# Two key tiles share one column-tiled pass for the second weighted sum of an attention backward

## The chip, the cores and the metric

One core of one Trainium2 chip runs the whole program in one launch. The metric is the device time in microseconds (us). The engines are TensorE (PE, with its weight loads shown apart as PEld), VectorE (DVE), ScalarE (ACT), GpSimd (POOL), and SyncE (SP), which here only issues DMAs.

## The reference

The program computes a forward pass and its vector-Jacobian product. The forward mixes two attentions over x (2048 tokens, width 576) with a gate:

```
q = (x @ wq) in 32 heads of 18;  k = x @ wk;  v = x @ wv      # one k and v for all heads
a = softmax(q k^T / sqrt(18)) v, heads joined, @ wo           # "A": multi-query attention
b = segment-recurrent attention with 8 memory tokens          # "B": 64 segments of 32 tokens, 32 heads of 128
out = g * a + (1 - g) * b,   g = sigmoid(x . gate_w)
```

The outputs are `out` and the gradients to x, to A's four weights, to B's memory and four weights and to the gate. For A's backward each query row needs the row sum l of its exponentials E = exp(s), the output o = (sum E v)/l, and delta = (sum E dP)/l with dP = dO v^T. The gradient to q is made from sum E dP k and sum E k. So with W = E * dP, element by element, each block of queries needs five sums over all 2048 keys: E times v, 1 and k, and W times 1 and k.

## The kernel before, in words

The stages run one after another: preparation and projections, a forward weave, B's backward in bulk, a backward weave, the weight gradients, and A's last products. The change is in the forward weave.

**The weave** (`weave`, L211) keeps the order of the code on each engine: it advances the chain by one piece, then the sweep by one step, 1024 times. The chain (`b_chain_fwd`, L237) is B's recurrence: 64 segments in 16 pieces each. Counted from 0, the pieces are: the k projection in two halves (0, 1), the transposes of k (2), the q projection (3, 4), the transposes of q (5), half of v (6), scores (7), their sums (8), the other half of v and the normalised weights c_pn (9), the transposes of v (10), weights times v with c_PB (11), and four pieces for the new memory (12 to 15). All pieces share two PSUM banks of one buffer each, c_pj and c_x. A projection half goes to c_pj and is evacuated by ACT (L63); the transposed k and q go to c_x and are evacuated by ACT (c_kmT, L308) and by DVE (c_qT, L334).

**The sweep** (`a_pass1`, L1372) goes over 64 blocks (16 pairs of heads x 4 groups of 512 queries) and, in each, over 16 key tiles of 128: 1024 steps, n = 0 to 1023. A step issues:

- the scores a_S of the next key tile for the pair's two heads (two row-tiled matmuls of 32 x 512; one buffer of two banks);
- a_dP for this key tile (two matmuls, two one-bank buffers in all);
- ACT's exponential of the next tile (a_E, L1394);
- two DVE products, one for each head, a_W = a_dP * a_E (L1424);
- the weighted sum of the step before's a_W into a_acc, and that of this step's a_E.

A weighted sum (`acc_mm`, L1396) is four matmuls, each with 32 weight columns and a 32-column group of the array of its own, so that the four run side by side:

```
for g in range(4):
    self.mm(acc[32 * g:32 * g + 32, :], lhsT=st[:, n % 16, 32 * (g % 2):32 * (g % 2) + 32],
            rhs=t[:, g // 2, :], start=first, stop=last, tp=(0, 32 * g))
```

The group g = 2 * head + half. The weights have 64 columns for a key tile, taken in two halves of 32: VK holds v, a column of ones and k (37 columns used), WK holds ones and k in columns 37 to 55. So WK's first half is all zeros, and E's and W's sums add into one accumulator of 64 rows for each head. a_acc has two buffers of one bank.

At a block's end (step n % 16 = 0 of the next block) ACT copies a_acc to SBUF (a_acs, L1429), and a generator `a_post` (L1453) goes on in three parts: at n % 16 = 1, four f32 transposes of a_acs to c_pj and ACT's copy a_tk; at 4, four transposes of the queries to c_pj and ACT's copy a_qt; at 6, a reciprocal on DVE, a row of small GpSimd operations, and three stores. All of it lies in the engines' queues in this order, between the chain's pieces.

Of the kernel before, what the change touches and what calls it, by code (L numbers as in the profile page):

```python
# [7 lines left out]
ALU = mybir.AluOpType  # L8
AX = mybir.AxisListType
BF16 = mybir.dt.bfloat16  # L10
F32 = mybir.dt.float32
P = 128
# [12 lines left out]
DA = 18  # L25
# [5 lines left out]
class Kern:  # L31
# [1142 lines left out]
    def setup_A_dram(self, dram):  # L1174
        T = self.T
        self.qd_dram = dram.tile([NPR, P, T], BF16, name="qd_dram")
        self.sd_dram = dram.tile([NPR, P, self.NTT, P], BF16, name="sd_dram")
        self.kv_dram = dram.tile([P, T], BF16, name="kv_dram")
        self.vk_dram = dram.tile([2, P, self.NTT, 64], BF16, name="vk_dram")
        self.dqtok_dram = dram.tile([T, D], BF16, name="dqtok_dram")  # L1180
        self.otok_dram = dram.tile([T, NKT * P], BF16, name="otok_dram")
        self.dkv_dram = dram.tile([P, T], BF16, name="dkv_dram")

    def setup_A_consts(self, pool):
        nc = self.nc
        om = pool.tile([P, 1], F32, name="a_onesrow")
        idx = [[0, 1]]
        nc.gpsimd.memset(om[:], 0.0)
        for r in (18, 50, 82, 83, 114, 115):
            nc.gpsimd.affine_select(out=om[:], in_=om[:], compare_op=ALU.not_equal, fill=1.0,  # L1190
                                    base=-r, pattern=idx, channel_multiplier=1)
        self.onesrow = om
        sel = pool.tile([P, 36], BF16, name="a_selkv")
        nc.gpsimd.memset(sel[:], 0.0)
        for i in range(4):
            w = i // 2
            nc.gpsimd.affine_select(out=sel[:, 18 * w:18 * w + DA], in_=sel[:, 18 * w:18 * w + DA],
                                    compare_op=ALU.not_equal, fill=1.0, base=-32 * i, pattern=[[-1, DA]],
                                    channel_multiplier=1)
        self.selkv = sel  # L1200

    def prep(self, keep, xk, sp, psum):
        nc = self.nc
# [90 lines left out]
    def a_setup(self, keep, sp, psum):  # L1294
        nc = self.nc
        T, NTT = self.T, self.NTT
        KV = keep.tile([P, T], BF16, name="a_KV")
        for lo in range(0, T, 512):
            pk = psum.tile([P, 512], F32, name="a_p1", bufs=2)
            for kt in range(NKT):  # L1300
                self.mm(pk[:, :], lhsT=self.wkv[:, kt, :], rhs=self.xT[:, kt, lo:lo + 512],
                        start=(kt == 0), stop=(kt == NKT - 1))
            nc.vector.tensor_scalar(out=KV[:, lo:lo + 512], in0=pk[:, :], scalar1=self.onesrow[:, 0:1],
                                    scalar2=None, op0=ALU.add)
        self.KV = KV
        nc.sync.dma_start(self.kv_dram[:, :], KV[:, :])
        absk = sp.tile([64, T], BF16, name="a_absk", bufs=1)
        nc.scalar.activation(absk[:, :], KV[0:64, :], ACT.Abs)
        mk = sp.tile([64, 1], F32, name="a_mk", bufs=1)
        nc.vector.tensor_reduce(out=mk[:, :], in_=absk[:, :], axis=AX.X, op=ALU.max)  # L1310
        sm = keep.tile([P, 64], BF16, name="a_smneg")
        nc.gpsimd.memset(sm[:], 0.0)
        for i in range(2):
            nc.gpsimd.memset(sm[32 * i:32 * i + DA, 32 * i + DA:32 * i + DA + 1], -1.0)
        nc.vector.tensor_scalar(out=sm[0:64, :], in0=sm[0:64, :], scalar1=mk[:, 0:1], scalar2=None, op0=ALU.mult)
        self.smneg = sm
        self.VK = keep.tile([P, NTT, 64], BF16, name="a_VK")
        self.WK = keep.tile([P, NTT, 64], BF16, name="a_WK")
        nc.gpsimd.memset(self.VK[:], 0.0)
        nc.vector.memset(self.WK[:], 0.0)  # L1320
        nc.gpsimd.memset(self.VK[:, :, DA:DA + 1], 1.0)
        nc.vector.memset(self.WK[:, :, 37:38], 1.0)
        for t4 in range(NTT // 4):
            pkv = psum.tile([P, 4, 36], F32, name="a_p2", bufs=2)
            for j in range(4):
                tt = t4 * 4 + j
                for kt in range(NKT):
                    rows = KT_ROWS[kt]
                    self.mm(pkv[:, j, :], lhsT=self.xT[0:rows, kt, tt * P:(tt + 1) * P],
                            rhs=self.wkv36[0:rows, kt, :], start=(kt == 0), stop=(kt == NKT - 1))  # L1330
            tts = slice(t4 * 4, t4 * 4 + 4)
            nc.vector.tensor_copy(self.VK[:, tts, 0:DA], pkv[:, :, DA:36])
            nc.vector.tensor_copy(self.VK[:, tts, 19:37], pkv[:, :, 0:DA])
            nc.scalar.copy(self.WK[:, tts, 38:56], pkv[:, :, 0:DA])
        nc.sync.dma_start(self.vk_dram[0], self.VK[:])
        nc.gpsimd.dma_start(self.vk_dram[1], self.WK[:])

    def load_A_kv(self, keep):
        nc = self.nc
        self.KV = keep.tile([P, self.T], BF16, name="l_KV")  # L1340
        nc.sync.dma_start(self.KV[:], self.kv_dram[:, :])
        self.VK = keep.tile([P, self.NTT, 64], BF16, name="l_VK")
        nc.sync.dma_start(self.VK[:], self.vk_dram[0])
        self.WK = keep.tile([P, self.NTT, 64], BF16, name="l_WK")
        nc.sync.dma_start(self.WK[:], self.vk_dram[1])

    def a_qd_all(self, sp, psum):
        prev = None
# [23 lines left out]
    def a_pass1(self, keep, sp, psum, xps):  # L1372
        nc = self.nc
        T, NTT = self.T, self.NTT
        NB = NPR * (T // 512)
        dl_all = keep.tile([P, NTT, NPR, 2, 2], BF16, name="a_dl")
        QD, S, E_, W_ = {}, {}, {}, {}
# [15 lines left out]
            E_[n] = sp.tile([P, 2, 512], BF16, name="a_E", bufs=2)  # L1393
            nc.scalar.activation(E_[n][:], S.pop(n)[:], ACT.Exp, scale=SCALEA)  # L1394

        def acc_mm(acc, n, src, st, first, last):  # L1396
            t = src.pop(n) if src is W_ else src[n]
            for g in range(4):
                self.mm(acc[32 * g:32 * g + 32, :], lhsT=st[:, n % 16, 32 * (g % 2):32 * (g % 2) + 32],
                        rhs=t[:, g // 2, :], start=first, stop=last, tp=(0, 32 * g))  # L1400

        load(0)
        load(1)
        mm_S(0)
        ex(0)
        NP_ = 16 * NB
        acc = None
        post = None
        for n in range(NP_ + 1):
            if n < NP_:  # L1410
                kt = n % 16
                if kt == 8:
                    load(n // 16 + 2)
                if n + 1 < NP_:
                    mm_S(n + 1)
                dP = [psum.tile([P, 512], F32, name="a_dP", bufs=2) for _ in range(2)]
                for i in range(2):
                    r = slice(64 + 32 * i, 96 + 32 * i)
                    self.mm(dP[i][:], lhsT=self.KV[r, kt * P:kt * P + P], rhs=QD[n // 16][r, :], tp=(64 + 32 * i, 0))
                if n + 1 < NP_:  # L1420
                    ex(n + 1)
                W_[n] = sp.tile([P, 2, 512], BF16, name="a_W", bufs=2)
                for i in range(2):
                    nc.vector.tensor_tensor(out=W_[n][:, i, :], in0=dP[i][:], in1=E_[n][:, i, :], op=ALU.mult)  # L1424
            if n > 0:
                acc_mm(acc, n - 1, W_, self.WK, False, n % 16 == 0)
                if n % 16 == 0:
                    acs = sp.tile([P, 512], F32, name="a_acs", bufs=1)
                    nc.scalar.copy(acs[:], acc[:])  # L1429
                    bb = n // 16 - 1  # L1430
                    post = self.a_post(bb // 4, bb % 4, acs, QD.pop(bb), sp, xps, dl_all)
            if n < NP_:
                if n % 16 == 0:
                    acc = psum.tile([P, 512], F32, name="a_acc", bufs=2)
                acc_mm(acc, n, E_, self.VK, n % 16 == 0, False)
            if post is not None and n % 16 in (1, 4, 6):
                if next(post, "end") == "end":
                    post = None
            yield
# [10 lines left out]
                    nc.sync.dma_start(self.qd_dram[p][82 + 32 * i:84 + 32 * i, t4 * 512:(t4 + 1) * 512],  # L1450
                                      dlT[4 * p + 2 * i:4 * p + 2 * i + 2, :])

    def a_post(self, p, qb, acs, QD, sp, psum, dl_all):  # L1453
        nc = self.nc
        pt = psum.tile([P, 4, P], F32, name="c_pj", bufs=1)
        for j in range(4):
# [3 lines left out]
        ptf = pt[:].rearrange("p a b -> p (a b)")  # L1460
        nc.scalar.copy(tkf, ptf)
        yield
        pd = psum.tile([P, 4, P], BF16, name="c_pj", bufs=1)
        for j in range(4):
            self.tr(pd[:, j, :], QD[:, j * P:(j + 1) * P], P)
# [4 lines left out]
        nc.vector.reciprocal(rl[:, :, 1, :], tk[:, :, :, 18])  # L1470
        nc.gpsimd.tensor_scalar(out=rl[:, :, 0, :], in0=rl[:, :, 1, :], scalar1=SCALEA, scalar2=None, op0=ALU.mult)
        dl = sp.tile([P, 4, 2], F32, name="a_d", bufs=2)
        nc.gpsimd.tensor_tensor(out=dl[:], in0=tk[:, :, :, 37], in1=rl[:, :, 1, :], op=ALU.mult)
        tts = slice(4 * qb, 4 * qb + 4)
        hi = sp.tile([P, 4, 2], BF16, name="a_dh", bufs=2)
        nc.gpsimd.tensor_scalar(out=hi[:], in0=dl[:], scalar1=-1.0, scalar2=None, op0=ALU.mult)
# [10 lines left out]
        nc.sync.dma_start(otd(self.otok_dram), ot[:].rearrange("p a b c -> p a (b c)"))  # L1487
        t1 = sp.tile([P, 4, 2, DA], F32, name="a_t1", bufs=1)
        nc.gpsimd.tensor_tensor(out=t1[:], in0=tk[:, :, :, 19:37], in1=bc(dl[:], DA), op=ALU.mult)
        nc.gpsimd.tensor_tensor(out=t1[:], in0=tk[:, :, :, 38:56], in1=t1[:], op=ALU.subtract)  # L1490
        dq = sp.tile([P, 4, 2, DA], BF16, name="a_dq", bufs=2)
        nc.gpsimd.tensor_tensor(out=dq[:], in0=t1[:], in1=bc(rl[:, :, 0, :], DA), op=ALU.mult)
        nc.sync.dma_start(otd(self.dqtok_dram), dq[:].rearrange("p a b c -> p a (b c)"))
# [305 lines left out]
```

## Time and profile before

| what | us |
|---|---|
| median of 3 runs (lowest, highest) | 6507.95 (6504.62, 6509.22) |
| the profiled execution | 6507.95 |
| its span in the trace | 6505.8 |
| PE busy, in the span | 5966.2 |
| DVE, ACT, POOL busy | 3772.9, 3492.4, 1961.9 |
| first to last a_S of the forward weave | 508.2 to 2462.0 |

Times in the profile are in us from the span's start, and the mean of one instruction is in ns. A group's line gives line number, engine, operation, out<-in with shapes, and the count; after the bar its busy time and the mean of one, then the idle time of the engine just before these instructions and what ended most of it. Busy time counts overlapping matmuls as one stretch, and a matmul's end is modelled, so the starts of PE's rows tell more than their lengths. In a timeline a row is start, length, engine, line, operation, tiles, count, and in brackets idle time with its releaser.

### The profile page before, as it was taken

What the parts mean: (1) busy time and instruction counts of PE and PEld (TensorE: products, weight loads), DVE (VectorE), ACT (ScalarE), POOL (GpSimd) and SP (SyncE); (2) the same over time, 40 slices, a digit from 0 to 9 for tenths busy, and PEclk for the clock granted to TensorE, in tenths of its full rate; (3) what the DMA queues carried; (4) which work ended last, traced back from release to release, by engine and by line L of the source; (5) the groups of instructions that cost most, each with busy time, mean ns of one, the idle gap of its engine ahead of it and who ended that gap; (6) DMA issues with size and microseconds to landing.
All of it is one profiled execution on the core that took longest, in us unless ns stands there. A gap on an engine that the chain in (4) does not pass through costs nothing. (4 is left out here: it accounts for less than half of the span.)

```text
span 6505.8 us, 208625 instructions
## 1 busy us (share of the span) xinstructions
PE 5966.2 (92%) x88611; PEld 3364.9 (52%) x88822; DVE 3772.9 (58%) x7061; ACT 3492.4 (54%) x5105; POOL 1961.9 (30%) x3451
## 2 busy tenths in 40 slices
PE   7898999999999994999969999999999899899996
PEld 5443444444444443877734444444444677675443
DVE  4336777777777773666658888888888211111111
ACT  3326777777777773666547777777777322211100
POOL 3003333333333333444423333333333111112212
PEclk9999999999999997999989999999999899999998
DMA  4636666766665445999864443444444899896643
GB/s 151 224 148 110 119 115 118 115 119 117 120 115 102 101 78 147 257 257 254 247 202 102 101 98 99 103 101 101 101 102 102 200 242 243 226 282 207 219 147 111
DMA packets 1368109, 991.95 MB, mean 152 GB/s; under 512 B 931613, under 2 KB 1184806, under 8 KB 1356486
## 3 DMA queue, kind: packets, MB, share of 16 engines
q1 hardware_dynamic: 1285030, 780.53, 50.8%
q0 software_dynamic: 82144, 198.05, 9.6%
q8 instruction: 696, 11.40, 0.8%
q14 instruction: 239, 1.96, 0.1%
HBM read 552.41 MB, written 384.76 MB: 144 GB/s over the span
## 5 line engine op out<-in xcount | busy, mean ns | idle before, releaser
L1424 DVE TENSOR_TENSOR a_W<-a_dP,a_E 128x512 bf16<-128x512 f32 x2048 | 1315.7, 684 | 470.1 <-PE a_dP L66 433.5
L1553 DVE TENSOR_TENSOR b_dS<-b_dP,b_E 128x512 bf16<-128x512 f32 x2048 | 1316.3, 685 | 325.0 <-PE b_dP L66 243.2
L1532 ACT ACTIVATE b_E<-b_S 128x1024 bf16<-128x1024 f32 x1024 | 1048.9, 1024 | 508.6 <-PE b_dP L66 360.8
L1394 ACT ACTIVATE a_E<-a_S 128x1024 bf16<-128x1024 f32 x1024 | 1051.0, 1026 | 169.1 <-PE a_dP L66 157.3
L66 PE MATMUL b_dP<-b_KV,b_QD 32*128 32x512 bf16 x2048 | 594.8, 380 | 5.4 <-DVE b_dS L1553 5.3
L66 PE MATMUL b_S<-b_KV,b_QD 32*128 32x512 bf16 x2048 | 399.6, 383 | 106.2 <-ACT b_E L1532 53.4
L66 PE MATMUL a_dP<-a_QD,l_KV 32*128 32x512 bf16 x2048 | 489.0, 382 | 0.9 <-DVE a_W L1424 0.7
L66 PE MATMUL w_acc<-w_d,w_h 128*128 128x512 bf16 (+1 forms) x2352 | 470.9, 379 | 2.5
L66 PE MATMUL r_pj<-WT,r_dT 128*32 128x288 bf16 x12288 | 444.0, 286 | 0.0
L66 PE MATMUL a_S<-a_QD,l_KV 32*128 32x512 bf16 x2048 | 398.7, 383 | 46.3 <-ACT a_E L1394 44.1
L66 PE MATMUL a_acc<-a_W,l_WK 128*32 128x512 bf16 x4096 | 409.9, 390 | 0.1
L66 PE MATMUL b_acc<-b_dS,b_SD 128*32 128x512 bf16 x2048 | 404.2, 391 | 0.0
L66 PE MATMUL b_acc<-b_E,b_SD 128*32 128x512 bf16 x2048 | 403.7, 391 | 0.0
L66 PE MATMUL a_acc<-a_E,l_VK 128*32 128x512 bf16 x4096 | 398.8, 379 | 0.0
L66 PEld LDWEIGHTS <-r_dT 128*32 128x32 bf16 x12288 | 329.1, 97 | 77.6 <-issue 0.3
L1027 DVE COPY y_T<-y_pt 128x512 bf16<-128x512 bf16 x256 | 97.3, 420 | 468.2 <-PE y_pt L71 450.1
L66 PEld LDWEIGHTS <-w_h 128*128 128x128 bf16 (+1 forms) x2400 | 213.1, 100 | 244.5 <-issue 3.4
L66 PEld LDWEIGHTS <-b_SD 128*32 128x32 bf16 x4096 | 105.2, 93 | 431.4 <-issue 430.3
L66 PEld LDWEIGHTS <-hm 128*32 128x32 bf16 x7680 | 206.4, 97 | 229.8 <-issue 14.5
L66 PEld LDWEIGHTS <-b_QD 32*128 32x128 bf16 x4096 | 140.3, 91 | 310.0 <-issue 215.9
L1013 ACT CAST y_tdk<-y_pk 128x512 bf16<-128x512 f32 x128 | 75.1, 587 | 379.6 <-PE y_pk L66 228.0
L66 PE MATMUL y_pdx<-WT,y_T 128*128 128x288 bf16 x2048 | 273.2, 287 | 0.0
(412 smaller groups left out, 11484.5 us busy)
## 6 DMA issues: line engine op xcount, KB each, us to landing
b_QD<-qd_dram SPq DMA_DIRECT2D x256, 128.0 KB
b_SD<-sd_dram SPq DMA_DIRECT2D x256, 128.0 KB
dOx_dram<-p_tok SPq DMA_DIRECT2D x16, 1024.0 KB
c_vx<-vx_dram SPq DMA_DIRECT2D x256, 64.0 KB
krow_dram<-c_k POOLq DMA_DIRECT2D x64, 256.0 KB, 2.5
qrow_dram<-c_q POOLq DMA_DIRECT2D x64, 256.0 KB, 3.1
vrow_dram<-c_v POOLq DMA_DIRECT2D x64, 256.0 KB, 4.1
x_q<-qx_dram SPq DMA_DIRECT2D x32, 512.0 KB
```

The lines of the kernel that those rows point to most:

```text
L66: return self.nc.tensor.matmul(out, lhsT, rhs, start=start, stop=stop, tile_position=tp, skip_group_check=True)
L1013: nc.scalar.copy(d[w][:, r, :], pk[:])
L1027: nc.vector.tensor_copy(T_[t][w][:], pt[:])
L1394: nc.scalar.activation(E_[n][:], S.pop(n)[:], ACT.Exp, scale=SCALEA)
L1424: nc.vector.tensor_tensor(out=W_[n][:, i, :], in0=dP[i][:], in1=E_[n][:, i, :], op=ALU.mult)
L1532: nc.scalar.activation(E_[n][:], S.pop(n)[:], ACT.Exp, scale=SCALEA)
L1553: nc.vector.tensor_tensor(out=D_[n][:, i, :], in0=dP[i][:], in1=E_[n][:, i, :], op=ALU.mult)
```

## The change

W's weighted sum gets an accumulator of its own, a_wacc, and is issued at even steps only, for two key tiles at once: the group g is now head g % 2 and key tile m + g // 2. The weights WK shrink to 32 columns for a tile (ones, k). The two key tiles' sums land in different rows of a_wacc (64 for each), and a selector matrix selw (128 x 64, f32) adds them when they are transposed. a_W has three buffers in place of two; a_acc and a_wacc have one each in place of a_acc's two. E's copy a_acs moves from step 0 of the next block to step 15. `a_post` gets a part: at the beginning of step 2, ahead of the step's matmuls and of its exponential, ACT copies a_wacc to SBUF (in the one buffer a_acs), and in step 4, ahead of the transposes of the queries, four f32 matmuls with selw go to c_x, and DVE copies them to a_tw. The GpSimd operations read a_tw where they read a_tk's columns 37 to 55.

```diff
-        self.vk_dram = dram.tile([2, P, self.NTT, 64], BF16, name="vk_dram")
+        self.vk_dram = dram.tile([P, self.NTT, 64], BF16, name="vk_dram")
+        self.wk_dram = dram.tile([P, self.NTT, 32], BF16, name="wk_dram")
...
+        sw = pool.tile([P, 64], F32, name="a_selw")
+        nc.gpsimd.memset(sw[:], 0.0)
+        for h in range(2):
+            nc.gpsimd.affine_select(out=sw[:], in_=sw[:], compare_op=ALU.not_equal, fill=1.0,
+                                    base=-64 * h, pattern=[[-1, 64]], channel_multiplier=1)
+        self.selw = sw
...
-            nc.scalar.copy(self.WK[:, tts, 38:56], pkv[:, :, 0:DA])
+            nc.scalar.copy(self.WK[:, tts, 1:19], pkv[:, :, 0:DA])
...
-        def acc_mm(acc, n, src, st, first, last):
-            t = src.pop(n) if src is W_ else src[n]
+        def acc_E(n):
             for g in range(4):
-                self.mm(acc[32 * g:32 * g + 32, :], lhsT=st[:, n % 16, 32 * (g % 2):32 * (g % 2) + 32],
-                        rhs=t[:, g // 2, :], start=first, stop=last, tp=(0, 32 * g))
+                self.mm(eacc[32 * g:32 * g + 32, :], lhsT=self.VK[:, n % 16, 32 * (g % 2):32 * (g % 2) + 32],
+                        rhs=E_[n][:, g // 2, :], start=(n % 16 == 0), stop=(n % 16 == 15), tp=(0, 32 * g))
+
+        def acc_W(m):
+            for g in range(4):
+                self.mm(wacc[32 * g:32 * g + 32, :], lhsT=self.WK[:, (m + g // 2) % 16, :],
+                        rhs=W_[m + g // 2][:, g % 2, :], start=(m % 16 == 0), stop=(m % 16 == 14), tp=(0, 32 * g))
...
         for n in range(NP_ + 1):
+            if post is not None and n % 16 == 2:
+                next(post)
...
-                W_[n] = sp.tile([P, 2, 512], BF16, name="a_W", bufs=2)
+                W_[n] = sp.tile([P, 2, 512], BF16, name="a_W", bufs=3)
...
-            if n > 0:
-                acc_mm(acc, n - 1, W_, self.WK, False, n % 16 == 0)
-                if n % 16 == 0:
-                    acs = sp.tile([P, 512], F32, name="a_acs", bufs=1)
-                    nc.scalar.copy(acs[:], acc[:])
...
+            if n > 0 and n % 2 == 0:
+                if n % 16 == 2:
+                    wacc = psum.tile([P, 512], F32, name="a_wacc", bufs=1)
+                acc_W(n - 2)
             if n < NP_:
                 if n % 16 == 0:
-                    acc = psum.tile([P, 512], F32, name="a_acc", bufs=2)
-                acc_mm(acc, n, E_, self.VK, n % 16 == 0, False)
+                    eacc = psum.tile([P, 512], F32, name="a_acc", bufs=1)
+                acc_E(n)
+                E_.pop(n - 1, None)
+                if n % 16 == 15:
+                    acs = sp.tile([P, 512], F32, name="a_acs", bufs=1)
+                    nc.scalar.copy(acs[:], eacc[:])
+                    bb = n // 16
+                    post = self.a_post(bb // 4, bb % 4, acs, wacc, QD.pop(bb), sp, xps, dl_all)
...
         nc.scalar.copy(tkf, ptf)
         yield
+        wcs = sp.tile([P, 512], F32, name="a_acs", bufs=1)
+        nc.scalar.copy(wcs[:], wacc[:])
+        yield
+        pw = psum.tile([P, 4, 64], F32, name="c_x", bufs=1)
+        for j in range(4):
+            self.mm(pw[:, j, :], lhsT=wcs[:, j * P:(j + 1) * P], rhs=self.selw[:, :])
+        tw = sp.tile([P, 4, 2, 32], F32, name="a_tw", bufs=1)
+        nc.vector.tensor_copy(tw[:].rearrange("p a b c -> p a (b c)"), pw[:])
         pd = psum.tile([P, 4, P], BF16, name="c_pj", bufs=1)
...
-        nc.gpsimd.tensor_tensor(out=dl[:], in0=tk[:, :, :, 37], in1=rl[:, :, 1, :], op=ALU.mult)
+        nc.gpsimd.tensor_tensor(out=dl[:], in0=tw[:, :, :, 0], in1=rl[:, :, 1, :], op=ALU.mult)
...
-        nc.gpsimd.tensor_tensor(out=t1[:], in0=tk[:, :, :, 38:56], in1=t1[:], op=ALU.subtract)
+        nc.gpsimd.tensor_tensor(out=t1[:], in0=tw[:, :, :, 1:19], in1=t1[:], op=ALU.subtract)
```

More of the change, by code (lines that the diff above doesn't have):

```diff
@@ L1317, in a_setup @@
         self.VK = keep.tile([P, NTT, 64], BF16, name="a_VK")
-        self.WK = keep.tile([P, NTT, 64], BF16, name="a_WK")
+        self.WK = keep.tile([P, NTT, 32], BF16, name="a_WK")
         nc.gpsimd.memset(self.VK[:], 0.0)
@@ L1321, in a_setup @@
         nc.gpsimd.memset(self.VK[:, :, DA:DA + 1], 1.0)
-        nc.vector.memset(self.WK[:, :, 37:38], 1.0)
+        nc.vector.memset(self.WK[:, :, 0:1], 1.0)
         for t4 in range(NTT // 4):
@@ L1333, in a_setup @@
             nc.vector.tensor_copy(self.VK[:, tts, 19:37], pkv[:, :, 0:DA])
-            nc.scalar.copy(self.WK[:, tts, 38:56], pkv[:, :, 0:DA])
-        nc.sync.dma_start(self.vk_dram[0], self.VK[:])
-        nc.gpsimd.dma_start(self.vk_dram[1], self.WK[:])
+            nc.scalar.copy(self.WK[:, tts, 1:19], pkv[:, :, 0:DA])
+        nc.sync.dma_start(self.vk_dram[:], self.VK[:])
+        nc.gpsimd.dma_start(self.wk_dram[:], self.WK[:])
     def load_A_kv(self, keep):
@@ L1342, in load_A_kv @@
         self.VK = keep.tile([P, self.NTT, 64], BF16, name="l_VK")
-        nc.sync.dma_start(self.VK[:], self.vk_dram[0])
-        self.WK = keep.tile([P, self.NTT, 64], BF16, name="l_WK")
-        nc.sync.dma_start(self.WK[:], self.vk_dram[1])
+        nc.sync.dma_start(self.VK[:], self.vk_dram[:])
+        self.WK = keep.tile([P, self.NTT, 32], BF16, name="l_WK")
+        nc.sync.dma_start(self.WK[:], self.wk_dram[:])
     def a_qd_all(self, sp, psum):
@@ L1394, in ex @@
             nc.scalar.activation(E_[n][:], S.pop(n)[:], ACT.Exp, scale=SCALEA)
-        def acc_mm(acc, n, src, st, first, last):
-            t = src.pop(n) if src is W_ else src[n]
+        def acc_E(n):
             for g in range(4):
-                self.mm(acc[32 * g:32 * g + 32, :], lhsT=st[:, n % 16, 32 * (g % 2):32 * (g % 2) + 32],
-                        rhs=t[:, g // 2, :], start=first, stop=last, tp=(0, 32 * g))
+                self.mm(eacc[32 * g:32 * g + 32, :], lhsT=self.VK[:, n % 16, 32 * (g % 2):32 * (g % 2) + 32],
[4 more added lines that the diff above has]
+                        rhs=W_[m + g // 2][:, g % 2, :], start=(m % 16 == 0), stop=(m % 16 == 14), tp=(0, 32 * g))
+            W_.pop(m)
+            W_.pop(m + 1)
         load(0)
@@ L1406, in a_pass1 @@
         NP_ = 16 * NB
-        acc = None
-        post = None
+        eacc = wacc = post = None
         for n in range(NP_ + 1):
+            if post is not None and n % 16 == 2:
+                next(post)
             if n < NP_:
@@ L1421, in a_pass1 @@
                     ex(n + 1)
-                W_[n] = sp.tile([P, 2, 512], BF16, name="a_W", bufs=2)
+                W_[n] = sp.tile([P, 2, 512], BF16, name="a_W", bufs=3)
                 for i in range(2):
                     nc.vector.tensor_tensor(out=W_[n][:, i, :], in0=dP[i][:], in1=E_[n][:, i, :], op=ALU.mult)
-            if n > 0:
-                acc_mm(acc, n - 1, W_, self.WK, False, n % 16 == 0)
-                if n % 16 == 0:
-                    acs = sp.tile([P, 512], F32, name="a_acs", bufs=1)
-                    nc.scalar.copy(acs[:], acc[:])
-                    bb = n // 16 - 1
-                    post = self.a_post(bb // 4, bb % 4, acs, QD.pop(bb), sp, xps, dl_all)
+            if n > 0 and n % 2 == 0:
+                if n % 16 == 2:
+                    wacc = psum.tile([P, 512], F32, name="a_wacc", bufs=1)
+                acc_W(n - 2)
             if n < NP_:
                 if n % 16 == 0:
-                    acc = psum.tile([P, 512], F32, name="a_acc", bufs=2)
-                acc_mm(acc, n, E_, self.VK, n % 16 == 0, False)
+                    eacc = psum.tile([P, 512], F32, name="a_acc", bufs=1)
[6 more added lines that the diff above has]
+                    post = self.a_post(bb // 4, bb % 4, acs, wacc, QD.pop(bb), sp, xps, dl_all)
             if post is not None and n % 16 in (1, 4, 6):
@@ L1451, in a_pass1, with a_post @@
                                       dlT[4 * p + 2 * i:4 * p + 2 * i + 2, :])
-    def a_post(self, p, qb, acs, QD, sp, psum, dl_all):
+    def a_post(self, p, qb, acs, wacc, QD, sp, psum, dl_all):
         nc = self.nc
```

## The prediction

> **What bounds the kernel now.** The diff touches the first of two "weaves": the recurrent chain (64 segments of 16 pieces) interleaved with the sweep `a_pass1` (64 blocks of 16 key tiles), one piece, then one sweep step. I call step k the sweep step with n % 16 = k; on TensorE the chain's piece k+1 follows it. I looked first at the costliest groups on the page, to find the operations edited:
>
> ```profile
> L1424 DVE TENSOR_TENSOR a_W<-a_dP,a_E 128x512 bf16<-128x512 f32 x2048 | 1315.7, 684 | 470.1 <-PE a_dP L66 433.5
> L66 PE MATMUL a_acc<-a_W,l_WK 128*32 128x512 bf16 x4096 | 409.9, 390 | 0.1
> ```
>
> The 410 us look like the prize, of which half is removed. They are not: busy time counts matmuls that overlap. Next, the busy time by stretch, for the weave alone:
>
> ```profile
> 508.00:2462.00 1954.00, 1870.76 (x33952) 880.58 (x33952) 1431.73 (x2552) 1428.35 (x1976) 696.63 (x1427) 1.00 0.60 110
> ```
>
> The columns are length, PE, weight loads, DVE, ACT, POOL, granted clock. 1954 us for 1024 steps is 1.91 us a step. PE is 96% busy at full clock, DVE and ACT 73%. Then TensorE's waits in this stretch (total us, times, longest):
>
> ```profile
> PE a_S L66 <- ACT a_E L1394: 43.8, 191, 1.1
> PE c_x L66 <- POOL c_PB L205: 32.6, 61, 1.5
> ```
>
> So some steps are not set by PE: the next scores wait for the exponential, because a_S has one buffer. Last, the order of time over one block's start:
>
> ```profile
> 1520.45 0.39 PE L66 MATMUL a_S<-a_QD,l_KV 32*128 32x512 bf16 x2
> 1520.57 0.59 ACT L63 CAST c_k<-c_pj 128x512 bf16<-128x512 f32 x1
> ...
> 1520.78 0.40 PE L66 MATMUL a_acc<-a_W,l_WK 128*32 128x512 bf16 x4
> ...
> 1521.01 0.39 PE L66 MATMUL a_acc<-a_E,l_VK 128*32 128x512 bf16 x4
> 1521.06 1.03 ACT L1394 ACTIVATE a_E<-a_S 128x1024 bf16<-128x1024 f32 x1
> ...
> 1521.33 0.66 PE L1457 MATMUL c_pj<-identF,a_acs 128*128 128x128 f32 x4
> ...
> 1521.82 0.61 PE L71 MATMUL c_x<-identB,c_k 128*128 128x128 bf16 x8
> 1522.07 0.59 ACT L1461 COPY a_tk<-c_pj 128x512 f32<-128x512 f32 x1
> ...
> 1522.36 0.39 PE L66 MATMUL a_S<-a_QD,l_KV 32*128 32x512 bf16 x2
> ...
> 1522.55 0.38 ACT L308 COPY c_kmT<-c_x 128x256 bf16<-128x256 bf16 x1
> ...
> 1522.84 1.02 ACT L1394 ACTIVATE a_E<-a_S 128x1024 bf16<-128x1024 f32 x1
> ...
> 1524.31 0.39 PE L66 MATMUL a_S<-a_QD,l_KV 32*128 32x512 bf16 x2
> ...
> 1526.81 0.39 PE L66 MATMUL a_acc<-a_E,l_VK 128*32 128x512 bf16 x4
> ...
> 1527.37 0.61 PE L71 MATMUL c_x<-identB,c_q 128*128 128x128 bf16 x8
> ...
> 1527.94 0.39 PE L66 MATMUL a_S<-a_QD,l_KV 32*128 32x512 bf16 x2
> ```
>
> These are steps 1, 2 (from 1522.36) and the end of 4. From W's first row to E's is 0.23 us: four column-tiled matmuls share the array and issue as one pass. Over all blocks its median is **0.226 us**, the price of one pass.
>
> I took the start-to-start times of a_S for each step position, medians over the blocks. They repeat to some hundredths, and fit three rules. A step is the larger of (a) PE's own order: 0.325 us of scores and dP, W 0.226, then E and the chain piece; (b) the exponential's loop: its start (0.43 to 0.60 us after a_S, later where a chain evacuation precedes it on ACT) + 1.025 + 0.05. And (c): the first weighted-sum pass starts no sooner than 2.177 us after the a_S of the step before, since dP's second buffer waits for VectorE's second product.
>
> **What the removed passes are worth.** The instruction order shows what it says: 2048 W matmuls in place of 4096, all on even steps. So each of 512 odd steps loses 0.226 us of PE, 116 us at most. By position, step time before in brackets:
> - 7 (1.551), 9 (1.682): rule b already decides. 0.
> - 15 (2.300), 3 (1.952): PE-bound; 0.226 each, kept.
> - 13 (1.657): down to b's 0.43 + 1.025 + 0.05 = 1.506; 0.151 kept.
> - 11 (1.746): falls to 1.555, but then c starts step 12's pass at 2.177 - 1.555 = 0.62 instead of 0.43. 0 net.
> - 1 (1.906): the f32 transposes wait for the c_k evacuation, at 0.70, so 1.79: 0.116. If step 2 did not wait anyway, c would return 0.06 of it.
> - 5 (2.123): 0.226.
>
> Together 0.226 x 3 + 0.151 + 0.054 = 0.88 us a block, x 64 = **56 us**, if all that is added were free. The Trainium skill, "TensorEngine Tiling (Array Packing)", section Theoretical Speedup, allows up to 4x for a small dimension of at most 32; going by that the removed passes pay their full 116 us. The rows above give half, because rules b and c take over.
>
> **What is added: each block's second accumulator.** W's sums no longer share a tile with E's, so each block also needs an ACT copy of a_wacc, four f32 selector matmuls into c_x, and a DVE copy.
>
> *Step 2.* The copy stands on ACT behind a_tk and c_kmT and ahead of the exponential; a_wacc has one buffer, and W's first pass of the new block, in this same step, waits for it. On PE everything is in order behind that pass. ACT operations overlap by 0.1 us. With step 1 at 1.79, a_tk starts 1.53 us after step 1's a_S, c_kmT 0.48 later, the copy 0.28 later, at 2.29, or 0.50 into step 2; with 0.592 (the a_acs row's mean) it ends at 1.09, and W starts at 1.14 instead of 0.325. Then 0.226 for W and 1.401 for E and the q projection: 2.77 in place of 1.952, **+0.82**. The exponential's loop ends at 0.98 + 1.08 = 2.06 and hides. Nearest bounds for the added wait: nothing (the copy done before W's pass) and 1.0 us (no overlap between ACT operations).
>
> *Step 4.* After E come the selector matmuls, then the c_q transposes (chain piece 5) into the same c_x, which has one buffer: PE waits for the DVE copy. No such matmul is in the trace; the nearest are these, and the copy's twin:
>
> ```profile
> 1512.50 0.61 PE L66 MATMUL c_x<-selF,c_hs 128*128 128x8 f32 x4
> ```
>
> ```profile
> L381 DVE CAST c_oT<-c_x 128x256 bf16<-128x256 f32 x64 | 27.2, 425 | 26.4 <-PE c_x L66 26.4
> ```
>
> Each selF matmul leaves two records (10 for 5 matmuls), issued 0.111 us apart. So four make 8 x 0.111 = 0.89 us. Below: f32 transposes, one record each, 0.109 apart: 0.44. Above: 64 moving columns not hidden behind weight loads, 0.158 each: 1.26. I take 0.89, the row with the same two records. Step 4's a_S is the origin: rule c puts W at 0.45 (step 3 is 1.727), E at 0.68, the selector at 1.00, its last result at 2.05, the DVE copy from 2.09 (the products end at 1.82) to 2.52, c_q's transposes at 2.57. From the first of those to the next a_S is 0.575 us (1527.37 to 1527.94). Step 4: about 3.15 for 1.682, **+1.48**. Its long interval frees step 5 of rule c, 0.17 more (2.123 to 1.726). ACT's a_qt copy and the chain's c_pj stay inside step 4.
>
> At nothing: the E copy moves to step 15, behind the exponential, and ends at the next step's a_S, before c_k's evacuation needs ACT; the wait for one a_acc buffer ends with it, before E's first pass at 0.55. Three a_W buffers, because two tiles are held. GpSimd's tail starts in step 6 as before, so c_PB's wait in step 10 stays. The prologue's two selects and the smaller WK store: within 3 us either way, beside other work there. Later stages are the same code.
>
> The skill's page just named, section PSUM Bottleneck, speaks against the change: tiling speeds TensorE but not the evacuation of PSUM. Counted as busy time, its two copies cost 1.0 us a block, about 65 us. The path here goes by waits, 2.3 us.
>
> **Sum.** Per block: step 15 -0.226, 1 -0.116, 2 +0.82, 3 -0.226, 4 +1.48, 5 -0.40, 13 -0.15, 11 and 12 zero: +1.17 us, x 63 or 64 = **+74 us**. The profiled execution ran 6507.95 us (span 6505.8 and 2.15 around it), which is also the median of the runs. Forecast **6582 us**, 1.1% slower; with the selector at its bounds 6565 (at 0.44 the DVE copy still waits for the products' end, 1.82) to 6606.
>
> **Rivals.**
> 1. *Slower, by less*: one of the two waits is hidden. For: both hang on ACT and DVE, 27% idle. Against: both are in order behind work that PE itself issues. Without step 2's: 6582 - 0.76 x 64 = 6533; with the selector alone on PE in step 4 (0.89, less the 0.12 idle there, no wait on the copy), 6537. Chance 0.12.
> 2. *Faster*: the post-processing stays beside other work, and the passes' 56 us remain: 6452. It decides from the point where steps 2 and 4 together add under 0.88 us a block (I find 2.3). For: the tail's ACT copies are hidden today. Against: a_wacc and c_x have one buffer each, and their next writer is the very next thing on PE. 0.05.
> 3. *Slower, by more*: the 64 columns take four cycles each behind every load, 0.218 a record: selector 1.74, 6636. Against: the f32 transposes hide 128 columns. 0.08.
> 4. *Nothing measurable*: waits and savings cancel, 6495 to 6521. 0.03.
>
> Forecast: 0.72. Range 6533 to 6622: it takes in rival 1 and the selector's bounds, not rivals 2 to 4. Within 0.2% (13 us) a measurement of this kernel can't tell from no change. Faster 0.05, same 0.03, slower 0.92.
>
> **What would show it.** Right: a PE wait of 0.6 to 0.8 us for ACT's a_wacc copy ahead of a_wacc's first pass, and of 0.4 to 0.6 for DVE's a_tw ahead of the c_q transposes, some 63 times each; steps 15, 3 and 13 shorter by 0.15 to 0.23; steps 7 and 9 unchanged; selector rows eight per block, 0.11 apart; the weave near 2028 us. Wrong: step 2 or 4 near its old time, or odd steps 7 and 9 shorter, which would mean that PE bound them.

## The result, and the profile after

The changed kernel took 6587.49 us (median of 4, 6582.89 to 6597.75) against 6506.28 us for the kernel before on the same chip: a ratio of 1.0128, 95% interval 1.011 to 1.0145. It is slower, by 81 us; 74 were forecast. The two profiled executions differ by 75 us.

The busy time of the forward weave, in the stretch from its first to its last a_S (length, PE, weight loads, DVE, ACT, POOL, clock, DMA):

```profile
505.00:2546.00 2041.00, 1873.91 (x32416) 913.87 (x32415) 1459.91 (x2615) 1461.88 (x2040) 698.34 (x1427) 1.00 0.56 105
```

The stretch is 87 us longer, with 1536 matmul records fewer on PE (2048 of passes gone, 64 x 8 of selectors new). PE's busy time hardly moved (1870.76 before): the selector's rows, 1.10 us in each of 64 blocks, put back about what the removed passes had taken. (Put back into the changed kernel, in the run zero_pass below, the passes add 62 us of busy time.) What PE waited for in that stretch (total, times, longest):

```profile
PE a_S L66 <- ACT a_E L1401: 59.2, 135, 1.1
PE a_wacc L66 <- ACT a_acs L1481: 43.2, 63, 0.9
PE c_x L66 <- POOL c_PB L205: 32.5, 62, 1.4
PE c_x L71 <- DVE a_tw L1487: 22.6, 63, 0.4
```

The second and the fourth row are new, 63 times each, 0.69 and 0.36 us at a time: the two waits that the prediction named (at 0.6 to 0.8 and 0.4 to 0.6 us, so the second is a little shorter than its sign). In order of time, the block that was shown for the kernel before (steps 2, 3 and 4 begin at 1531.57, 1534.33 and 1536.27):

```profile
1531.57 0.39 PE L66 MATMUL a_S<-a_QD,l_KV 32*128 32x512 bf16 x2
...
1531.76 0.40 ACT L308 COPY c_kmT<-c_x 128x256 bf16<-128x256 bf16 x1
...
1532.03 0.62 ACT L1481 COPY a_acs<-a_wacc 128x512 f32<-128x512 f32 x1
...
1532.70 0.40 PE L66 MATMUL a_wacc<-a_W,l_WK 128*32 128x512 bf16 x4 [0.68 <-ACT a_acs L1481]
...
1534.33 0.39 PE L66 MATMUL a_S<-a_QD,l_KV 32*128 32x512 bf16 x2
...
1534.44 0.59 ACT L63 CAST c_q<-c_pj 128x512 bf16<-128x512 f32 x1 [0.86 <-PE c_pj L66]
...
1535.08 1.26 PE L66 MATMUL c_pj<-Wq,hm 128*32 128x512 bf16 x20
...
1537.14 1.10 PE L66 MATMUL c_x<-a_selw,a_acs 128*128 128x64 f32 x8
...
1538.35 0.42 DVE L1487 COPY a_tw<-c_x 128x256 f32<-128x256 f32 x1 [0.26 <-PE c_x L66]
...
1538.83 0.61 PE L71 MATMUL c_x<-identB,c_q 128*128 128x128 bf16 x8 [0.36 <-DVE a_tw L1487]
...
1539.37 0.39 PE L66 MATMUL a_S<-a_QD,l_KV 32*128 32x512 bf16 x2
```

The copy of a_wacc stands behind c_kmT, and W's pass starts 1.13 us into step 2 (1.14 forecast). The selector's eight records last 1.10 us, and c_q's transposes start 2.56 us into step 4 (2.57 forecast).

All steps, as medians over the blocks of the time from one a_S to the next, worked out from the traces (in the column "forecast", "same" is a step that the prediction left as it was; the last four columns are experiments, told below; bold marks what the text goes back to):

| step | before | forecast | after | early_copy | sel_step3 | zero_pass | split_tail10 |
|---|---|---|---|---|---|---|---|
| 0 | 1.953 | same | 1.953 | 1.953 | 1.952 | 1.952 | 1.953 |
| 1 | 1.906 | 1.79 | 1.792 | 1.793 | 1.792 | 1.906 | 1.792 |
| 2 | 1.952 | 2.77 | 2.761 | **2.012** | 2.761 | 2.741 | 2.011 |
| 3 | 1.952 | 1.73 | **1.946** | 1.951 | 2.885 | 1.952 | 1.951 |
| 4 | 1.682 | 3.15 | 3.097 | 3.098 | **1.682** | 3.098 | 1.677 |
| 5 | 2.123 | 1.73 | 1.735 | 1.736 | 1.907 | 1.952 | 1.911 |
| 6 | 1.682 | same | 1.739 | 1.739 | 1.681 | 1.682 | 1.682 |
| 7 | 1.551 | same | 1.554 | 1.554 | 1.552 | 1.551 | 1.551 |
| 8 | 2.251 | same | 2.250 | 2.250 | 2.250 | 2.250 | 2.251 |
| 9 | 1.682 | same | 1.682 | 1.682 | 1.682 | 1.682 | 1.692 |
| 10 | 2.108 | same | 2.108 | 2.107 | 2.106 | 2.107 | 1.553 |
| 11 + 12 | 4.140 | same | 4.140 | 4.140 | 4.140 | 4.141 | 4.186 |
| 13 | 1.657 | 1.506 | 1.509 | 1.509 | 1.509 | 1.656 | 1.509 |
| 14 | 1.505 | same | 1.502 | 1.502 | 1.503 | 1.504 | 1.502 |
| 15 | 2.300 | 2.07 | 2.083 | 2.083 | 2.083 | 2.300 | 2.084 |

### The profile page after: what moved, and what is told of

Same layout as the page of the kernel before. It is cut to its first block, busy times and chain, and to the rows that moved or that the text cites. A ratio compares the mean times of both kernels' runs of the same rounds, so it can differ in the third digit from the quotient of the medians.

```text
span 6580.8 us, 205751 instructions
## 1 busy us (share of the span) xinstructions
PE 5973.7 (91%) x87075; PEld 3402.2 (52%) x87286; DVE 3800.1 (58%) x7125; ACT 3527.5 (54%) x5169; POOL 1964.9 (30%) x3454
## 5 line engine op out<-in xcount | busy, mean ns | idle before, releaser
L66 PE MATMUL a_dP<-a_QD,l_KV 32*128 32x512 bf16 x2048 | 508.1, 382 | 0.9 <-DVE a_W L1438 0.7
L66 PE MATMUL a_S<-a_QD,l_KV 32*128 32x512 bf16 x2048 | 399.1, 384 | 61.2 <-ACT a_E L1401 59.2
L636 POOL TENSOR_TENSOR x_P<-x_E,x_r 128x512 bf16<-128x512 bf16 x128 | 133.3, 1041 | 433.3 <-DVE x_r L633 351.3
```

Source lines behind the costliest of these rows:

```text
L66: return self.nc.tensor.matmul(out, lhsT, rhs, start=start, stop=stop, tile_position=tp, skip_group_check=True)
L636: nc.gpsimd.tensor_tensor(out=o[:, r, :], in0=Et[:, :, lo:lo + n], in1=rl[:].unsqueeze(2).to_broadcast([P, 4, n]), op=ALU.mult)
```

## The experiments

The theory: the weave's time follows the prediction's three step rules, the passes pay only where PE ends a step last, and the loss sits in two waits behind tiles of one buffer (a_wacc in step 2, c_x in step 4) and in the selector matmuls. The rival, "PE work": the weave runs at the speed of TensorE's matmuls, added and removed, and a wait only shifts idle time.

Beside the experiments the kernel before took 6487 to 6489 us, where it took 6506 beside the first run of the changed one, so totals are compared as ratios, each to the kernel before beside it, and the sizes of effects by the weave, from first to last a_S: 1953.8 us before, 2039.8 after. The rest of the span, whose code is the same, came out at 4528 to 4552 us in the profiles of this study; single totals are no finer than that.

**The changed kernel once more.**

> The changed kernel as it is, once more beside the kernel before on one chip, so that the other runs' differences can be read against it. Both theories: 1.0128 of before, with the weave some 86 us longer.

6577.56 us, ratio 1.0135 (1.0121 to 1.0149), weave 2041.3 us: the same kernel twice differs by 1.5 us of weave.

**early_copy.**

```diff
-            if post is not None and n % 16 == 2:
-                next(post)
...
-            if post is not None and n % 16 in (1, 4, 6):
+            if post is not None and n % 16 in (0, 1, 4, 6):
...
+        wcs = sp.tile([P, 512], F32, name="a_wcs", bufs=1)
+        nc.scalar.copy(wcs[:], wacc[:])
+        yield
         pt = psum.tile([P, 4, P], F32, name="c_pj", bufs=1)
```

> The changed kernel with the ScalarE copy of a_wacc issued at the end of step 0 into a buffer of its own instead of at the head of step 2 (room for it: two a_QD buffers instead of three, one each of a_ot and a_dq). Theory of waits (the loss sits in two waits behind one-buffer tiles): PE no longer waits for the copy in step 2, which goes from 2.76 to 2.01 us (rule c leaves 0.06 over the old 1.95), nothing else moves; 0.75 x 63 = 47 us less than the changed kernel's 6587, so 6540 us. Rival theory of PE work (the weave runs at the speed of PE's added and removed matmuls, and a wait only shifts idle time): the same matmuls, so no change, 6587 us.

Ratio 1.0071 (1.0056 to 1.0086); weave 1995.1 us, 44.7 less than after. Step 2 is 2.012 us, no other step moved by more than 0.005, and the wait is gone. TensorE's waits:

```profile
PE a_S L66 <- ACT a_E L1401: 59.2, 135, 1.1
PE c_x L66 <- POOL c_PB L205: 33.3, 64, 1.4
PE c_x L71 <- DVE a_tw L1484: 22.7, 63, 0.4
```

The copy has nearly the same length (0.59 us against 0.62) at another place and in a tile of its own, so what cost the time was its place. PE work expected nothing: it falls.

**sel_step3.** The selector's part of `a_post` gets a `yield` of its own behind it:

```diff
+        yield
         pd = psum.tile([P, 4, P], BF16, name="c_pj", bufs=1)
...
-            if post is not None and n % 16 in (1, 4, 6):
+            if post is not None and n % 16 in (1, 3, 4, 6):
```

> The changed kernel with the selector matmuls and VectorE's copy a_tw at the end of step 3 instead of in step 4, so that the next writer of c_x (the c_q transposes after step 4) finds it free. Theory of waits: step 3 takes the matmuls, 1.95 to 2.8 us; step 4 falls from 3.10 to 1.68, as rule b has it; step 5 pays 0.16 to rule c again, step 6 gives back 0.06: 0.45 us a block, 28 us less, 6559 us. Rival of PE work: the same matmuls at another place, 6587 us.

Ratio 1.0114 (1.0099 to 1.0129); weave 2020.2 us, 19.5 less. Steps 4, 5 and 6 did what was expected; step 3 grew by 0.94 instead of 0.85. In the trace, the selector begins 0.655 us into step 3, its eight records are issued 0.11 apart, and the column-tiled projection starts 0.20 after the last of them, at 1.69 instead of 0.750. The expectation had not reckoned this change of form. Step 4 gave back what was expected; the matmuls in step 3 cost a little more, so that 19.5 us were saved and not 28.

**zero_pass.**

```diff
+            if wacc is not None and n % 2 == 1:
+                for g in range(4):
+                    self.mm(wacc[32 * g:32 * g + 32, :], lhsT=self.zeros[:, 0:32], rhs=W_[n - 1][:, g % 2, :],
+                            start=False, stop=True, tp=(0, 32 * g))
             if n < NP_:
                 if n % 16 == 0:
```

> The changed kernel with the removed pass put back: at each odd step four column-tiled matmuls of zero weights with a_W add nothing to a_wacc. Theory of waits (step rules): back come 0.22 us in step 15, 0.11 in step 1 (its f32 transposes wait for c_k's evacuation), nothing in 3 (the second half of the q projection waits for c_q's evacuation anyway), 0.23 in 5 (of which 6 gives back 0.06), 0.15 in 13, nothing net in 7, 9 and 11 with 12: 0.65 us a block, 42 us, so 6629 us. Rival of PE work: 512 x 0.226 = 116 us, 6703 us.

Ratio 1.0203 (1.0186 to 1.022); weave 2081.6 us, 41.8 more than after. The removed pass is worth 42 us where its issue time is 512 x 0.226 = 116: it costs 0.22 us in steps 5 and 15, 0.15 in 13, 0.11 in 1 and nothing in 3, 7 and 9; steps 6 and 2 give back 0.06 and 0.02, and what it adds to step 11 it takes from 12.

**before_tail12.**

```diff
-            if post is not None and n % 16 in (1, 4, 6):
+            if post is not None and n % 16 in (1, 4, 12):
```

> The kernel before with only the last part of the post-processing (a reciprocal, GpSimd's operations and the stores) moved from step 6 to step 12. Theory of waits: GpSimd gets to c_PB 0.25 us sooner (it was still busy with a_qt when c_v was evacuated, and two DMA issues of 1.15 us and c_PB's own 1.08 follow), so that PE's wait in step 10 falls from 0.5 to about 0.25 us: 0.25 x 63 = 16 us less than before's 6506, 6490 us. Rival of PE work: no matmul is touched, 6506 us.

Ratio 1.0009 (0.9999 to 1.0018); weave 1947.9 us, 5.9 less. The total shows no gain. In the weave the direction is right and the size a third: step 10 fell to 2.028, by 0.08 instead of 0.25, and in seven blocks step 5 grew, by 4.4 us in all (in five of them TensorE waits behind ACT's a_qt, 3.1 us; split_sel, below, has the same wait). In one block of this run, the end of step 8 and steps 9 and 10 (start, length, operation): DVE makes c_PB's input c_pn, and later GpSimd makes c_PB.

```profile
1532.87 0.28 DVE L366 TENSOR_TENSOR c_pn<-c_E,c_rd 128x128 bf16<-128x128 bf16 x1
...
1534.33 0.54 POOL L298 DMA_DIRECT2D vrow_dram<-c_v  x1 [8.75 <-ACT c_v L63]
1534.86 0.54 POOL L367 DMA_DIRECT2D pm_dram<-c_pn  x1
1535.42 1.09 POOL L205 TENSOR_TENSOR c_PB<-c_pn,bmask 128x512 bf16<-128x512 bf16 x1
```

GpSimd idles 8.75 us, and c_PB, whose input has been ready since 1533.15, still stands behind the issue of c_v's rows, which waits for ACT's c_v. The tail was hardly in its way; the order on GpSimd was.

**before_pb** and **split_sel.** The first moves these two DMA issues behind c_PB:

```diff
-            rows_out("v")
             pn = sp.tile([P, 2, 64], BF16, name="c_pn", bufs=1)
...
-            nc.gpsimd.dma_start(self.pm_dram[s], pn[:].rearrange("p a b -> p (a b)"))
             PB = sp.tile([P, 16, 4, 8], BF16, name="c_PB", bufs=1)
             self.expand(PB[:], pn[:].rearrange("p a (u q) -> p (a u) q", q=8), 16)
+            rows_out("v")
+            nc.gpsimd.dma_start(self.pm_dram[s], pn[:].rearrange("p a b -> p (a b)"))
```

> The kernel before with one reordering in the chain: in piece 9 GpSimd makes c_PB before it issues the DMAs of c_v's rows and of c_pn, instead of after (in the run with the late tail c_PB still stood behind these two, which wait for c_v's evacuation). Theory of waits: c_PB is ready before PE asks for it; step 10 falls from 2.11 to about 1.6 us; rule c then moves part of that into step 11 (plus 0.27) and takes 0.1 off step 12; 0.35 us a block, 22 us less than before. Rival of PE work: no matmul is touched, no change.

Ratio 0.9962 (0.9948 to 0.9976); weave 1926.4 us, 27.5 less than before. Step 10 is 1.552, 11 rose to 2.045 and 12 fell to 2.288, the way that rule c was expected to move them; 22 us were expected. The rival's "no change" falls again.

split_sel is early_copy and before_pb together with the selector in two halves:

```diff
+        tw = sp.tile([P, 4, 2, 32], F32, name="a_tw", bufs=1)
+        for hf, nm in ((0, "c_pj"), (1, "c_x")):
+            pw = psum.tile([P, 2, 64], F32, name=nm, bufs=1)
+            for j in range(2):
+                jj = 2 * hf + j
+                self.mm(pw[:, j, :], lhsT=wcs[:, jj * P:(jj + 1) * P], rhs=self.selw[:, :])
+            nc.vector.tensor_copy(tw[:, 2 * hf:2 * hf + 2].rearrange("p a b c -> p a (b c)"), pw[:])
+            yield
...
-            if post is not None and n % 16 in (0, 1, 4, 6):
+            if post is not None and n % 16 in (0, 1, 4, 7, 9, 12):
```

> The changed kernel with both waits taken away and the added matmuls put where PE is idle: the early copy of a_wacc (end of step 0, own buffer), two selector matmuls at the end of step 7 into c_pj and two at the end of step 9 into c_x, each with a DVE copy of its half, the last part of the post-processing at step 12, and GpSimd's reordering of the run before_pb. Theory of waits, by the step rules: step 2 2.01, 3 1.95, 4 1.68, 5 1.91, 7 1.55, 9 about 1.72, 10 1.55, 11 1.82, 12 2.32, 13 1.51, 15 2.08: 29.3 us a block against before's 30.44, 74 us less than before (ratio 0.989), and some 50 us less than before_pb. Rival of PE work: after's 1.0128, since all its matmuls are there.

Ratio 0.9917 (0.9905 to 0.993); weave 1887.6 us, 66 less than before and 39 less than before_pb, where 74 and some 50 were expected. The medians of the 16 steps add to 29.26 us (29.3 expected), but step 5's mean, 2.09 us, lies above its median, 1.91: in 16 blocks it is longer, by 12 us in all.

**split_tail10.** In split_sel's list of steps, 12 becomes 10.

> split_sel with the last part of the post-processing at step 10 instead of 12, right behind c_PB on GpSimd. In split_sel step 5 is 1.91 us in its median but 2.09 in its mean: a_qt has one buffer, its store is issued late, and in some 16 of 63 blocks ScalarE's next a_qt copy in step 4 waits for it, with the v projection behind it. Theory of waits: the store leaves two steps, some 4 us, sooner, most of these waits go, 0.18 x 63 = 11 us less than split_sel: ratio to before 0.990. Rival (the waits come from other transfers that hold the DMA queues): no change, 0.9917.

Ratio 0.9915 (0.9901 to 0.9928); weave 1881.3 us, 6.3 less than split_sel. Step 5's mean is 1.906: those waits are gone; the store of a_qt now leaves 25 us after the start of its post-processing block instead of 35. Step 12 gave 0.05 us back and the intervals of the two totals overlap, so the 11 us are shown in step 5 alone. It beats the kernel before and the changed one. TensorE's longest waits in its weave, where the first had been 43.8 us before and 59.2 after:

```profile
PE a_S L66 <- ACT a_E L1401: 4.0, 10, 1.1
PE c_pj L66 <- DMA hm<-in_B_mem_dram: 3.5, 3, 3.1
```

**split_zero.** The diff of zero_pass on split_tail10.

> split_tail10 with the removed pass put back at each odd step, as four column-tiled matmuls of zero weights with a_W that add nothing. By the step rules the pass is worth more in this arrangement than in the changed kernel, where it cost 42 us: back come 0.22 in step 15, 0.11 in 1, 0.21 in 5, 0.22 in 7 and 0.23 in 9 (their idle time now holds the selector matmuls), 0.20 in 11 and 12 together, 0.15 in 13: 1.33 us a block, 85 us more than split_tail10. If the pass is worth in any arrangement what it was worth before: 42 us. If PE work alone counts: 116 us.

Ratio 1.0007 (0.9999 to 1.0016); weave 1939.1 us, 57.8 more than split_tail10. Neither 42 nor 85 nor 116. Steps 1, 5, 9, 13 and 15 paid as expected (0.11, 0.21, 0.22, 0.15, 0.22) and 11 with 12 0.15; but step 7 paid 0.14, not 0.22, and rule c gave 0.14 back in step 8 and 0.06 in step 2. So in this arrangement the pass is worth 58 us, half of its issue time.

## Why the prediction was right, and where it was not

*What bounds the weave*: shown. The rules and the two waits gave 11 of the 16 steps to 0.02 us (six of them as unchanged) and the sum of steps 11 and 12, and early_copy, sel_step3 and zero_pass moved just the steps that they should.

*What the passes are worth*: 56 us were forecast with everything else free; zero_pass measures 42 in the changed kernel, split_zero 58 where the additions are hidden. That 58 lies near 56 is luck: it is made of other steps (nothing in 3, but 0.22 in 9, where the selector stands in that run). In the changed kernel steps 7 and 9 gave nothing and step 11 gave its gain to 12, as said.

*Step 3, "0.226 kept"*: wrong, and the largest term missed. Step 3 stayed at 1.946. c_pj has one buffer: the second half of the q projection (1535.08 in the timeline, 0.75 into the step) waits for ACT's evacuation of the first (1534.44 and 0.59 long, so to 1535.03). The prediction had found this wait in step 1, where it holds the f32 transposes, and had not looked for it in step 3, where the removed pass had just covered it (the projection started 0.767 into the step before). 0.22 x 64 = 14 us.

*Step 6, at nothing*: 0.057 too low. As step 5 became shorter, rule c started step 6's W later (0.443 into the step, as 2.177 - 1.735 gives; 0.325 by PE's own order), and step 6 has too little idle PE time to hide it.

*Step 2, +0.82*: 0.809 measured. The copy began 0.04 us sooner and lasted 0.03 longer than reckoned. early_copy shows that the wait is the cause.

*Step 4, +1.48*: 1.415 measured. That c_q's transposes started when forecast (2.56 for 2.57) is in part luck. With step 3 longer than forecast, rule c no longer delayed W, and the selector began at 0.87 instead of 1.00; but from there to the start of the DVE copy it took 1.21 us instead of 1.09 (the first two records lie 0.16 apart, the others 0.112). The copy took the 0.424 us reckoned, and the next a_S came 0.54 us after the transposes' start instead of 0.575. The row with two records for each f32 matmul was the right one; no run shows the 0.158 or the 0.218 us a record of the upper bound and of rival 3. That the c_x wait and not the matmuls alone cost the time, sel_step3 shows.

*The sum*: 1.41 us a block by the step medians (1.34 by the means, which take in the first block, where the copies and the selector are absent, and a few long steps), where 1.17 were forecast; the weave grew by 86 us, not 74. (The prediction's terms add to 1.18, and 3.15 for 1.682 is +1.47, not +1.48; neither matters.) The profiled executions differ by only 75 us because the rest of the span was 11 us shorter (4541 against 4552), which lies within what that unchanged code does from run to run: so near an agreement of the total is chance.

*The rivals*: "slower, by less" falls, both waits are there in full; so do "slower, by more", with records 0.11 us apart, and "nothing measurable". "Faster" needed both waits off the path: split_sel made that come true, by moving the work, and got it. Its net gain over before_pb is 39 us of weave (45 in split_tail10, without the long steps 5), below the 56 of rival 2: step 3 gives nothing, and step 2 takes back 0.06 us by rule c.

*The Trainium skill*, "TensorEngine Tiling (Array Packing)", section Theoretical Speedup, allows up to four times for 32 columns. That is a figure for tiling itself, which no run here varies; it does not say what a removed pass returns. The runs show 42 and 58 us of the 116 that the passes issue. Its section PSUM Bottleneck warned of evacuation, and the trace agrees in kind: 43.2 and 22.6 us of PE's waits are for the two evacuations. But early_copy kept the first copy and lost its wait, and split_sel kept both and lost both waits.

## What to carry to other kernels

In a kernel whose work is woven by hand, price a removed instruction step by step: it pays only where its engine ends the step last, and here a third to a half of it was kept. An added evacuation of a one-buffer tile costs little as work and much as a wait if the tile's next writer is the next thing in an in-order queue; put it far enough ahead of that writer (here, at the end of step 0 for a writer in step 2). And look at what stands in a queue ahead of a short operation that someone waits for: moving GpSimd's c_PB ahead of two DMA issues took 27 us off the weave of the kernel before.

## What the runs showed of the hardware

GpSimd's work beside a DVE operation can lengthen it, here by two thirds in the median and fourfold at most. c_pn, a DVE product of 128 x 128 bf16 values from two SBUF tiles, has this row (minimum, median and maximum in ns) in the kernel before, where a_post's GpSimd operations a_dq and a_qt run beside it in all but one or two of the 64 segments:

```profile
L366 DVE TENSOR_TENSOR c_pn<-c_E,c_rd x64: 282/466/1172, 527.9 to 2452.2; 128x128 bf16<-128x128 bf16 x64
```

and this in before_tail12, where no GpSimd operation runs beside it:

```profile
L366 DVE TENSOR_TENSOR c_pn<-c_E,c_rd x64: 281/282/283, 527.0 to 2446.1; 128x128 bf16<-128x128 bf16 x64
```

The skill's page "SBUF — State Buffer", section Who interferes with whom, says that a DVE instruction with two SBUF inputs contends with a GpSimd instruction that reads SBUF; the rows agree. Here it cost no time that shows: in the kernel before, c_pn ended at least 1.16 us before c_PB, its reader, began.

An f32 matmul with 128 weight columns and 64 moving ones left two records and took 0.22 us of issue (8 records, 0.112 apart after a first gap of 0.160), the same as with 8 moving columns (0.11 apart). In sel_step3, going from it to column-tiled bf16 matmuls took 0.20 us after its last record.
